# A retention-then-feed-forward kernel on one core: loads reordered between two DMA queues, weight columns interleaved, the first output block computed earlier

## The chip, the cores and the metric

The kernel runs on one core of a Trainium2 chip. The metric is the device time of one execution in microseconds (us), and the median of several runs is what counts.

## The reference

There are two parts, run one after the other. The first is a linear recurrence per batch entry and head (retention): a 64x64 state decays by a constant factor per head, takes up the outer product of k and v of each step, and is read by q. The second is a feed-forward block on all 3072 tokens.

```
q, k, v: (4, 8, 768, 64) f32;  gamma_h = 1 - 2**(-5-h)
state = gamma_h * state + k_t (outer) v_t
y_t = (1/8) * q_t @ state
x = y as (4*768, 512)
h = x @ w_in            # (512, 2048)
out = (h * cos(h)) @ w_out   # (2048, 512), f32
```

## The kernel before

The recurrence is done in chunks of 128 steps. A "pair" p (12 of them, `NP`) is one chunk of two batch entries with all 8 heads: pairs 0 to 5 are the six chunks of the first two entries, 6 to 11 those of the other two. Two pairs make a "group" g of 512 tokens (6 of them, `NG`), and a group is the unit of the feed-forward block.

Work on one pair, with the names of the code: `load` (L105) brings q, k and v for both entries from DRAM, six DMAs of 256 KB in fp32. `conv_q`, `conv_k`, `conv_v` (L150 to L165) scale them and make them bf16. `stage_t` (L167) transposes q and k on TensorE (PE) through a PSUM bank, 16 small matmuls, and copies the result to `qkt`; `stage_t_dma` (L183) does the same with two DMA transposes from the SP queue instead, and is used from pair `PT` on. `stage_a` (L196) makes the scores, 16 matmuls; `stage_m` (L211) masks them on VectorE (DVE). `stage_y` (L219) makes the outputs and the new state, and copies the outputs to `xt`, the input of the feed-forward block.

The feed-forward block has two products. F is x times `w_in`, then h*cos(h) by a Sin on ScalarE (ACT, L258) and a product on DVE (L262) into `gt`. `unit_f` (L264) does one block f of 128 of the 2048 hidden columns for the 512 tokens of a group: four matmuls of 512 columns. `pair_f` (L272) does four blocks (4r to 4r+3) for the 256 tokens of one pair: sixteen matmuls of 256 columns each; it can start when only one pair of the group is done. O is `gt` times `w_out`: `unit_o(g, j, part)` (L288) does a quarter (`part`) of the sum over f for token block j in four matmuls; after part 3 ACT copies the bank out and SP stores it.

The schedule is written out by hand: each engine runs its instructions in exactly the order in which the code issues them. There are two DMA queues for the loads: the one fed by SP ("hardware queue") and the one fed by GpSimd ("software queue", POOL). The weights come by the software queue, `w_in` in slices of 512 of its 2048 columns (L114; the first slice as two halves), `w_out` in four slices of 512 rows (L119), and are cast to bf16 on the way. Waits between engines, and for DMAs, are put in by the framework from the memory ranges that the instructions touch. It gives each queue eight DMA semaphores in rotation, so a ninth DMA of a queue is issued when the first has landed.

The order of the first third (L311 to L389): pairs 0 and 1 with idle-filling matmuls (`warm`, L313); F of both in part r=0; F of group 0 for r=1, 2, 3 as pair parts; pair 2; F of pair 2 with pair 3 between; F of pair 3. From L393 on is a loop over groups: in turn one unit of F of group g, one unit of O of group g-1, with the stages of the next pairs put between at fixed steps. The first round (g=1) has no F, only the O of group 0 with pairs 4 and 5; the second (g=2) has F of group 2 and O of group 1, and so on.

Of the kernel before, what the change touches and what calls it, by code (L numbers as in the profile page):

```python
# [30 lines left out]
def kernel(  # L31
# [9 lines left out]
    nc = tc.nc  # L41
# [8 lines left out]
    NP = B // 2 * NC  # L50
    NG = NP // 2
    PRE = 5
    PT = 5

    scale = 1.0 / math.sqrt(D)
    lg = [math.log(1.0 - 2.0 ** (-5.0 - h)) for h in range(H)]
# [48 lines left out]
    def load(eng, p, names):  # L105
        bp, c = divmod(p, NC)
        for n in names:
            t, src = SRC[n[0]]
            b = int(n[1])
            eng.dma_start(  # L110
                out=t[p % PRE][b],
                in_=src[2 * bp + b, :, ds(c * C, C)].rearrange("h t d -> t h d"))

    def load_w_in(r, n=512):  # L114
        nc.gpsimd.dma_start(
            out=w_in_sb[:, :, ts(r, n)],
            in_=moe_w_in[:, ts(r, n)].rearrange("(i p) f -> p i f", p=128))

    def load_w_out(r):  # L119
        nc.gpsimd.dma_start(  # L120
            out=w_out_sb[:, ts(r, 4), :],
            in_=moe_w_out[ts(r, 512), :].rearrange("(f p) m -> p f m", p=128))


    nc.gpsimd.iota(pos, pattern=[[C, NC]], base=1, channel_multiplier=1,
                   allow_small_or_imprecise_dtypes=True)
    load(nc.sync, 0, ("q0", "k0", "q1"))
    load(nc.sync, 1, ("q0", "q1"))
    load(nc.gpsimd, 0, ("k1", "v0", "v1"))
    make_identity(nc, ident)  # L130
    nc.vector.memset(zero, 0.0)
    nc.vector.memset(lnsc, math.log(scale))
# [17 lines left out]
    def conv_q(p, eng):  # L150
        for b in range(2):
            eng.tensor_tensor(out=qs[p % NB][:, b], in0=qf[p % PRE][b],  # L152
                              in1=bc(gq, p % NC), op=ALU.mult)

    def conv_v(p, eng):
        for b in range(2):
            eng.tensor_tensor(out=vs[p % NB][:, b], in0=vf[p % PRE][b],  # L157
                              in1=bc(gk, p % NC), op=ALU.mult)

    def conv_k(p, on_act):  # L160
        for b in range(2):
            if on_act:
                nc.scalar.copy(out=ks[p % NB][:, b], in_=kf[p % PRE][b])  # L163
            else:
                nc.vector.tensor_copy(out=ks[p % NB][:, b], in_=kf[p % PRE][b])  # L165

    def stage_t(p, split, fill=0):  # L167
        n = p % NB
        for b in range(2):
            if fill:  # L170
                warm(fill * b)
            bank = banks.take()
            tr = bank.bitcast(BF16).rearrange("p (w a t) -> p w a t", w=2, a=HP)
            for w, src in enumerate((qs[n], ks[n])):
                for a in range(HP):
                    nc.tensor.transpose(tr[:, w, a, :], src[:, b, 2 * a : 2 * a + 2, :], ident)  # L176
            if split is None or split and b == 1:
                nc.vector.tensor_copy(out=qkt[n][:, :, b], in_=tr)  # L178
            else:
                nc.scalar.copy(out=qkt[n][:, :, b], in_=tr)  # L180
            banks.give(bank)

    def stage_t_dma(p):  # L183
        n = p % NB
        for w, src in enumerate((qs[n], ks[n])):
            nc.sync.dma_start_transpose(
                out=qkt[n][:, w].rearrange("p b a t -> p (b a) t"),
                in_=src.rearrange("p b h d -> p (b h d)"))
# [75 lines left out]
    def unit_f(g, f):  # L264
        bank = banks.take()
        for i in range(KIN):
            nc.tensor.matmul(bank, lhsT=w_in_sb[:, i, ts(f, 128)], rhs=xt[g % 2][:, i, :],  # L267
                             start=(i == 0), stop=(i == KIN - 1))
        act(bank, gt[g % 2][:, f, :])
        banks.give(bank)  # L270

    def pair_f(p, r, parts=(0, 1)):  # L272

        g, hf = divmod(p, 2)
        for f in [4 * r + 2 * i for i in parts]:
            bank = banks.take()
            for e in range(2):
                for i in range(KIN):
                    nc.tensor.matmul(bank[:, ts(e, 256)], lhsT=w_in_sb[:, i, ts(f + e, 128)],  # L279
                                     rhs=xt[g % 2][:, i, ts(hf, 256)],  # L280
                                     start=(i == 0 and e == 0), stop=(i == KIN - 1),
                                     skip_group_check=True)
            act(bank, gt[g % 2][:, f : f + 2, ts(hf, 256)])
            banks.give(bank)
# [2 lines left out]

    def unit_o(g, j, part):  # L288
        if part == 0:
            o_bank[0] = banks.take()  # L290
        bank = o_bank[0]
        for f in range(4 * part, 4 * part + 4):
            nc.tensor.matmul(bank, lhsT=gt[g % 2][:, f, ts(j, 128)], rhs=w_out_sb[:, f, :],  # L293
                             start=(f == 0), stop=(f == KOUT - 1))
        if part == 3:
            o = ob[j % 4]
            bp, c = divmod(2 * g + j // 2, NC)
            dst = out[ds((2 * bp + j % 2) * S + c * C, C), :]
            if g == NG - 1 and j == 3:
                nc.vector.tensor_copy(out=o[:, ts(0, 256)], in_=bank[:, ts(0, 256)])  # L300
                nc.sync.dma_start(out=dst[:, ts(0, 256)], in_=o[:, ts(0, 256)])
                nc.scalar.copy(out=o[:, ts(1, 256)], in_=bank[:, ts(1, 256)])
                nc.scalar.dma_start(out=dst[:, ts(1, 256)], in_=o[:, ts(1, 256)])
            else:
                nc.scalar.copy(out=o, in_=bank)  # L305
                nc.sync.dma_start(out=dst, in_=o)
            banks.give(bank)
# [5 lines left out]
    def warm(n):  # L313
        for _ in range(n):
            nc.tensor.matmul(spare, lhsT=zero[:, :128], rhs=zero, start=True, stop=True,
                             skip_group_check=True)

    def masks(p, items):
        for it in items:
            stage_m(p, it)  # L320

    load(nc.gpsimd, 1, ("k0", "k1", "v0", "v1"))
    load_w_in(0, 256)
    load_w_in(1, 256)
    for r in (1, 2, 3):
        load_w_in(r)
    for p in (2, 3, 4):
        load(nc.sync, p, ("q0", "q1", "v0"))
    conv_v(1, nc.gpsimd)
    load(nc.gpsimd, 2, ("k0", "k1", "v1"))  # L330
    load(nc.gpsimd, 3, ("k0", "k1"))
    conv_q(2, nc.gpsimd)
    load(nc.gpsimd, 3, ("v1",))
    load_w_out(0)
    conv_v(2, nc.gpsimd)
    load_w_out(1)

    warm(10)
    conv_q(0, nc.vector)
# [7 lines left out]
    conv_q(1, nc.vector)  # L347
    warm(6)
    stage_y(0, nc.scalar.copy)
    conv_q(3, nc.gpsimd)  # L350
    load_w_out(2)
    load_w_out(3)
    conv_v(3, nc.gpsimd)
    load(nc.gpsimd, 4, ("k0", "k1", "v1"))
    stage_t(1, None)
    m1 = stage_a(1)
    masks(1, m1)
# [1 line left out]
    banks.give(spare)  # L359
    stage_y(1, nc.scalar.copy)  # L360
    pair_f(1, 0)
    for r in (1, 2, 3):
        pair_f(0, r)
        pair_f(1, r)
    conv_k(2, True)
    stage_t(2, None)
    m2 = stage_a(2)
    masks(2, m2)
    stage_y(2, nc.scalar.copy)
    load(nc.sync, 5, ("q0", "q1", "v0"))  # L370
    conv_q(4, nc.gpsimd)
    load(nc.gpsimd, 5, ("k0", "k1", "v1"))
    pair_f(2, 0)
    conv_k(3, True)
    pair_f(2, 1)
    stage_t(3, None)
    pair_f(2, 2, (0,))
    m3 = stage_a(3)
    masks(3, m3)
    pair_f(2, 2, (1,))  # L380
    pair_f(2, 3)
    stage_y(3, nc.scalar.copy)
    conv_v(4, nc.gpsimd)
    load(nc.sync, 6, ("q0", "q1", "v0"))
    load(nc.gpsimd, 6, ("k0", "k1", "v1"))
    for r in range(4):
        pair_f(3, r)
        if r == 2:
            conv_k(4, True)  # L389


    todo = []
    for g in range(1, NG + 1):  # L393
        for s in range(16):
            hf, r = divmod(s, 8)
            p = 2 * (g + 1) + hf
            if 1 < g < NG:
                unit_f(g, s)
            unit_o(g - 1, *divmod(s, 4))
            if p < NP:  # L400
                if r == 0 and p + 1 < NP:
                    conv_q(p + 1, nc.gpsimd)
                    conv_k(p + 1, True)
                    conv_v(p + 1, nc.gpsimd)
                elif r == 1 and p < PT:
                    stage_t(p, False)
                elif r == 2:
                    todo = stage_a(p)
                    stage_m(p, todo[0])
                    if PT <= p + 1 < NP:  # L410
                        stage_t_dma(p + 1)
                elif r == 3:
                    stage_m(p, todo[1])
                elif r == 6:
                    stage_y(p)
                    if p + 3 < NP:
                        load(nc.sync, p + 3, ("q0", "q1", "v0"))
                        load(nc.gpsimd, p + 3, ("k0", "k1", "v1"))


# [28 lines left out]
```

## Time and profile before

| what | value |
|---|---|
| median of 7 runs | 220.09 us |
| lowest and highest | 219.76 and 221.34 us |
| time of the profiled execution | 220.22 us |
| span of its trace | 218.5 us |
| mean granted TensorE clock over the span | 0.992 |
| busy PE, DVE, ACT, POOL | 92%, 52%, 53%, 38% |
| software queue (q0), hardware queue (q1) | 13.90 MB, 19.01 MB |

The span runs from the first instruction of the program to the last; 1.7 us of the execution lie around it. "Busy" of PE counts pipelined matmuls at their modelled length, so what PE loses is better seen in the distance from the start of one matmul to the start of the next. In the trace, lines such as L279 are lines of the kernel before.

### The profile page before, as it was taken

The page shows a single profiled execution, that of the slowest core. Times are in us where ns is not written, and L with a number is a line of the kernel's source. Part 1 is how long each engine was busy: PE and PEld are TensorE (multiplying, and loading weights), DVE is VectorE, ACT ScalarE, POOL GpSimd, SP SyncE. Part 2 cuts the span into 40 slices and gives each one's busy share as a digit, 9 for nine tenths or more (in the row PEclk, how much of TensorE's full clock was granted, in tenths as well). Part 3 has the DMA queues.
Part 4 walks back from the last instruction along what each step waited for, and adds up shares of the span by engine and source line. Part 5 has one row for each costly group of instructions (what it writes and reads, how often), then busy time and mean ns, then how long its engine had stood idle before and what let it go on. Part 6 is the DMA issues. An engine that isn't in the chain of part 4 may idle for free.

```text
span 218.5 us, 4249 instructions
## 1 busy us (share of the span) xinstructions
PE 201.7 (92%) x1679; PEld 112.5 (51%) x1699; DVE 113.5 (52%) x183; ACT 116.1 (53%) x185; POOL 83.9 (38%) x96
## 2 busy tenths in 40 slices
PE   7578996889999999999999999999999999999992
PEld 2246884768855454544544544544544544444440
DVE  4398588386663416557447547547546244333000
ACT  5654874748874274564474564564534644454120
POOL 7989432598799863946330520000000000000000
PEclk9799999999999999999999999999999999999999
DMA  6999999899999999998851651051011001110221
GB/s 162 330 246 196 212 314 224 172 177 282 307 207 304 293 193 314 253 231 207 206 143 52 148 144 48 3 144 50 3 48 48 20 31 48 48 49 4 96 85 59
DMA packets 62516, 33.31 MB, mean 152 GB/s; under 512 B 52320, under 2 KB 57184, under 8 KB 62496
## 3 DMA queue, kind: packets, MB, share of 16 engines
q1 hardware_dynamic: 54640, 19.01, 38.7%
q0 software_dynamic: 7712, 13.90, 25.6%
q8 instruction: 13, 0.21, 0.4%
q10 hardware_dynamic: 144, 0.13, 0.2%
q14 instruction: 7, 0.06, 0.1%
HBM read 27.26 MB, written 6.29 MB: 154 GB/s over the span
## 4 chain that ended last, share of the span: by engine, by line
PE 82%; DVE 6%; ACT 5%; DMA 3%; issue 2%; SPq 0%; DVEq 0%; ACTq 0%
PE bank L293 37%; PE bank L267 25%; PE bank L279 11%; DMA qf<-in_q_dram 3%; PE bank L205 3%; DVE am L214 2%; PE bank L228 2%; PE bank L233 2%; ACT cosb L258 1%; ACT ks L163 1%; DVE qkt L178 1%; DVE qs L152 1%; ACT xt L237 1%; PE bank L176 1%; DVE gt L262 1%
## 5 line engine op out<-in xcount | busy, mean ns | idle before, releaser
L262 DVE TENSOR_TENSOR gt<-bank,cosb 128x512 bf16<-128x512 f32 x96 | 65.9, 690 | 70.1 <-ACT cosb L258 70.0
L258 ACT ACTIVATE cosb<-bank,halfpi 128x512 bf16<-128x512 f32 x96 | 65.7, 687 | 60.1 <-PE bank L267 49.9
L293 PE MATMUL bank<-w_out_sb,gt 128*128 128x512 bf16 x377 | 93.5, 379 | 0.6 <-issue 0.3
L267 PE MATMUL bank<-xt,w_in_sb 128*128 128x512 bf16 x244 | 64.2, 379 | 1.3 <-issue 0.9
L293 PEld LDWEIGHTS <-gt 128*128 128x128 bf16 x384 | 37.2, 98 | 44.3
L267 PEld LDWEIGHTS <-w_in_sb 128*128 128x128 bf16 x256 | 24.1, 98 | 28.3
L214 DVE TENSOR_TENSOR am<-bank,mask 128x512 bf16<-128x512 f32 x48 | 30.2, 681 | 5.9 <-PE bank L205 3.3
L152 POOL TENSOR_TENSOR qs<-qf,gq 128x512 bf16<-128x512 f32 x20 | 20.6, 1051 | 31.5 <-DMA qf<-in_q_dram 29.0
L279 PE MATMUL bank<-xt,w_in_sb 128*128 128x256 bf16 x256 | 28.9, 273 | 1.4 <-ACT xt L237 1.4
L279 PEld LDWEIGHTS <-w_in_sb 128*128 128x128 bf16 x256 | 24.8, 98 | 4.4 <-issue 1.3
L157 POOL TENSOR_TENSOR vs<-vf,gk 128x512 bf16<-128x512 f32 x22 | 23.0, 1062 | 7.4 <-DMA vf<-in_v_dram 7.4
L305 ACT COPY ob<-bank 128x512 f32<-128x512 f32 x23 | 13.5, 585 | 16.3 <-PE bank L293 16.3
L110 POOL DMA_DIRECT2D kf<-in_k_dram x23 | 20.9, 912 | 0.4 <-issue 0.4
L237 ACT CAST xt<-bank 128x512 bf16<-128x512 f32 x24 | 13.1, 588 | 14.6 <-PE bank L233 14.6
L163 ACT CAST ks<-kf 128x512 bf16<-128x512 f32 x24 | 13.7, 615 | 2.6 <-DMA kf<-in_k_dram 2.6
L233 PE MATMUL bank<-am,vs 128*64 128x128 bf16 x192 | 12.2, 220 | 1.2 <-DVE am L214 1.1
L110 POOL DMA_DIRECT2D vf<-in_v_dram x14 | 12.4, 890 | 0.0
L250 DVE CAST stb<-st_ps 64x512 bf16<-64x512 f32 x12 | 8.3, 689 | 6.5 <-PE st_ps L245 6.3
L233 PEld LDWEIGHTS <-vs 128*64 128x64 bf16 x192 | 10.3, 110 | 1.8 <-issue 1.1
L228 PEld LDWEIGHTS <-stb 128*64 128x64 bf16 x160 | 8.7, 109 | 4.5 <-issue 4.2
L228 PE MATMUL bank<-qkt,stb 128*64 128x128 bf16 x160 | 10.6, 222 | 0.0
L205 PE MATMUL bank<-qkt 64*128 64x128 bf16 x192 | 8.4, 222 | 2.3 <-DVE qkt L178 1.9
(37 smaller groups left out, 68.6 us busy)
## 6 DMA issues: line engine op xcount, KB each, us to landing
qf<-in_q_dram SPq DMA_DIRECT2D x24, 256.0 KB, 6.5
kf<-in_k_dram POOLq DMA_DIRECT2D x23, 256.0 KB, 5.3
out_dram<-ob SPq DMA_DIRECT2D x23, 256.0 KB, 2.1
vf<-in_v_dram POOLq DMA_DIRECT2D x14, 256.0 KB, 6.2
vf<-in_v_dram SPq DMA_DIRECT2D x10, 256.0 KB, 7.0
w_out_sb<-in_moe_w_out_dram POOLq DMA_DIRECT2D x4, 512.0 KB, 8.9
w_in_sb<-in_moe_w_in_dram POOLq DMA_DIRECT2D x3, 512.0 KB, 14.3
w_in_sb<-in_moe_w_in_dram POOLq DMA_DIRECT2D x2, 256.0 KB, 8.0
```

Of the source, the lines that this page charges most:

```text
L110: eng.dma_start(out=t[p % PRE][b], in_=src[2 * bp + b, :, ds(c * C, C)].rearrange("h t d -> t h d"))
L152: eng.tensor_tensor(out=qs[p % NB][:, b], in0=qf[p % PRE][b], in1=bc(gq, p % NC), op=ALU.mult)
L157: eng.tensor_tensor(out=vs[p % NB][:, b], in0=vf[p % PRE][b], in1=bc(gk, p % NC), op=ALU.mult)
L163: nc.scalar.copy(out=ks[p % NB][:, b], in_=kf[p % PRE][b])
L214: nc.vector.tensor_tensor(out=am[p % 2][b][j], in0=ap[j], in1=mask.unsqueeze(1).to_broadcast([128, HP, 128]), op=ALU.mult)
L228: nc.tensor.matmul(yp[ts(j, 64), a, :], lhsT=stb[p % 2][:, b, a, ts(j, 64)], rhs=qt(n, b, a), start=True, stop=False, skip_group_check=True)
L233: nc.tensor.matmul(yp[ts(j, 64), a, :], lhsT=vs[n][:, b, 2 * a + j, :], rhs=am[p % 2][b][j][:, a, :], start=(c == 0), stop=True, skip_grou ...
L258: nc.scalar.activation(out=cb, in_=bank, func=AF.Sin, bias=halfpi)
L262: nc.vector.tensor_tensor(out=out, in0=bank, in1=cb, op=ALU.mult)
L267: nc.tensor.matmul(bank, lhsT=w_in_sb[:, i, ts(f, 128)], rhs=xt[g % 2][:, i, :], start=(i == 0), stop=(i == KIN - 1))
L279: nc.tensor.matmul(bank[:, ts(e, 256)], lhsT=w_in_sb[:, i, ts(f + e, 128)], rhs=xt[g % 2][:, i, ts(hf, 256)], start=(i == 0 and e == 0), s ...
L293: nc.tensor.matmul(bank, lhsT=gt[g % 2][:, f, ts(j, 128)], rhs=w_out_sb[:, f, :], start=(f == 0), stop=(f == KOUT - 1))
```

## The change

- **Layout of the weights.** Hidden columns are now numbered so that block f (with r = f // 4, j = f % 4) is made of the columns 512 r + 4 m + j, m = 0..127. `w_out` rows follow the same numbering, so that a partition of a `w_out` slice takes four neighbouring rows, 8 KB in one piece of DRAM, where it took four pieces of 2 KB. `w_in_sb` is filled as before, and its weight operands are read with a step of four elements through the new `w_in_t`.
- **Loads.** At the start SP issues v0 of pair 1 in place of q1 of pair 1, which goes to POOL; `iota` comes after POOL's first load. `w_in` is loaded in four slices, and all four `w_out` slices follow it on POOL, ahead of k and v of the pairs 2 to 4. For pairs 3 and 4 v0 also moves from SP to POOL.
- **Order of the work.** F of group 0 for f = 4..15 is done in `unit_f` form. O of group 0 comes right after it, ahead of and between the stages of pair 2, with two `o_bank`s at a time for j = 0, 1. The round g=1 of the loop is gone: pairs 4 and 5 with the first eight units of O of group 1 are written out ahead of the loop, and the round g=2 has the other eight at every second step. `conv_q` and `conv_v` of pair 2 and `conv_q` of pair 3 go from POOL to DVE. Two `warm` matmuls are added after pair 0. `PT` is 4, so pair 4 is transposed by DMA and no longer on PE.

```diff
-    PT = 5
+    PT = 4
...
-            in_=moe_w_out[ts(r, 512), :].rearrange("(f p) m -> p f m", p=128))
+            in_=moe_w_out[ts(r, 512), :].rearrange("(p j) m -> p j m", j=4))
+
+    w_in_f = w_in_sb.rearrange("p i (r m j) -> p i r j m", r=4, j=4)
+
+    def w_in_t(i, f):
+        return w_in_f[:, i, f // 4, f % 4, :]
...
-    load(nc.sync, 1, ("q0", "q1"))
-    load(nc.gpsimd, 0, ("k1", "v0", "v1"))
+    load(nc.sync, 1, ("q0", "v0"))
+    load(nc.sync, 2, ("q0", "q1", "v0"))
+    load(nc.gpsimd, 0, ("k1",))
...
+    load(nc.gpsimd, 0, ("v0", "v1"))
...
-            nc.tensor.matmul(bank, lhsT=w_in_sb[:, i, ts(f, 128)], rhs=xt[g % 2][:, i, :],
+            nc.tensor.matmul(bank, lhsT=w_in_t(i, f), rhs=xt[g % 2][:, i, :],
...
-                    nc.tensor.matmul(bank[:, ts(e, 256)], lhsT=w_in_sb[:, i, ts(f + e, 128)],
+                    nc.tensor.matmul(bank[:, ts(e, 256)], lhsT=w_in_t(i, f + e),
...
-    load(nc.gpsimd, 1, ("k0", "k1", "v0", "v1"))
-    load_w_in(0, 256)
-    load_w_in(1, 256)
-    for r in (1, 2, 3):
+    load(nc.gpsimd, 1, ("k0", "q1", "k1", "v1"))
+    for r in range(4):
         load_w_in(r)
-    for p in (2, 3, 4):
-        load(nc.sync, p, ("q0", "q1", "v0"))
     conv_v(1, nc.gpsimd)
+    for r in range(4):
+        load_w_out(r)
+    load(nc.sync, 3, ("q0", "q1"))
     load(nc.gpsimd, 2, ("k0", "k1", "v1"))
-    load(nc.gpsimd, 3, ("k0", "k1"))
-    conv_q(2, nc.gpsimd)
-    load(nc.gpsimd, 3, ("v1",))
-    load_w_out(0)
-    conv_v(2, nc.gpsimd)
-    load_w_out(1)
+    load(nc.gpsimd, 3, ("k0", "k1", "v0", "v1"))
+    load(nc.sync, 4, ("q0", "q1"))
+    load(nc.gpsimd, 4, ("k0", "k1", "v0", "v1"))
...
     pair_f(1, 0)
-    for r in (1, 2, 3):
-        pair_f(0, r)
-        pair_f(1, r)
+    for f in range(4, 16):
+        unit_f(0, f)
+
     conv_k(2, True)
+    conv_q(2, nc.vector)
+    conv_v(2, nc.vector)
+    for part in range(4):
+        for j in range(2):
+            unit_o(0, j, part)
+    unit_o(0, 2, 0)
+    unit_o(0, 2, 1)
     stage_t(2, None)
+    unit_o(0, 2, 2)
     m2 = stage_a(2)
     masks(2, m2)
+    conv_k(3, True)
+    unit_o(0, 2, 3)
...
+    for part in range(3):
+        unit_o(0, 3, part)
     stage_y(2, nc.scalar.copy)
+    unit_o(0, 3, 3)
+    conv_q(3, nc.vector)
...
+    attend(4)
+    o_units(1, 0, 4)
+    later(4)
+    attend(5)
+    ahead(6)
+    stage_t_dma(6)
+    o_units(1, 4, 8)
+    later(5)
```

More of the change, by code (lines that the diff above doesn't have):

```diff
@@ L121, in load_w_out @@
             out=w_out_sb[:, ts(r, 4), :],
-            in_=moe_w_out[ts(r, 512), :].rearrange("(f p) m -> p f m", p=128))
+            in_=moe_w_out[ts(r, 512), :].rearrange("(p j) m -> p j m", j=4))
+    w_in_f = w_in_sb.rearrange("p i (r m j) -> p i r j m", r=4, j=4)
+    def w_in_t(i, f):
+        return w_in_f[:, i, f // 4, f % 4, :]
+    load(nc.sync, 0, ("q0", "k0", "q1"))
+    load(nc.sync, 1, ("q0", "v0"))
+    load(nc.sync, 2, ("q0", "q1", "v0"))
+    load(nc.gpsimd, 0, ("k1",))
     nc.gpsimd.iota(pos, pattern=[[C, NC]], base=1, channel_multiplier=1,
                    allow_small_or_imprecise_dtypes=True)
-    load(nc.sync, 0, ("q0", "k0", "q1"))
-    load(nc.sync, 1, ("q0", "q1"))
-    load(nc.gpsimd, 0, ("k1", "v0", "v1"))
+    load(nc.gpsimd, 0, ("v0", "v1"))
     make_identity(nc, ident)
@@ L289, in unit_o @@
         if part == 0:
-            o_bank[0] = banks.take()
-        bank = o_bank[0]
+            o_bank[j] = banks.take()
+        bank = o_bank[j]
         for f in range(4 * part, 4 * part + 4):
@@ L349 @@
     stage_y(0, nc.scalar.copy)
[L350 to L354, printed above, removed]
+    warm(2)
     stage_t(1, None)
@@ L361, with attend, ahead, later @@
     pair_f(1, 0)
-    for r in (1, 2, 3):
-        pair_f(0, r)
-        pair_f(1, r)
+    for f in range(4, 16):
+        unit_f(0, f)
     conv_k(2, True)
+    conv_q(2, nc.vector)
[5 more added lines that the diff above has]
+    unit_o(0, 2, 1)
     stage_t(2, None)
+    unit_o(0, 2, 2)
     m2 = stage_a(2)
     masks(2, m2)
+    conv_k(3, True)
+    unit_o(0, 2, 3)
+    load(nc.sync, 5, ("q0", "q1", "v0"))
+    load(nc.gpsimd, 5, ("k0", "k1", "v1"))
+    for part in range(3):
+        unit_o(0, 3, part)
     stage_y(2, nc.scalar.copy)
-    load(nc.sync, 5, ("q0", "q1", "v0"))
+    unit_o(0, 3, 3)
+    conv_q(3, nc.vector)
+    conv_v(3, nc.gpsimd)
     conv_q(4, nc.gpsimd)
-    load(nc.gpsimd, 5, ("k0", "k1", "v1"))
+    conv_v(4, nc.gpsimd)
     pair_f(2, 0)
-    conv_k(3, True)
+    stage_t(3, None)
     pair_f(2, 1)
-    stage_t(3, None)
-    pair_f(2, 2, (0,))
     m3 = stage_a(3)
     masks(3, m3)
-    pair_f(2, 2, (1,))
+    conv_k(4, True)
+    stage_t_dma(4)
+    load(nc.sync, 6, ("q0", "q1", "v0"))
+    load(nc.gpsimd, 6, ("k0", "k1", "v1"))
+    pair_f(2, 2)
     pair_f(2, 3)
     stage_y(3, nc.scalar.copy)
[L383 to L386, printed above, removed]
-        pair_f(3, r)
[L388 to L393, printed above, removed]
+    conv_q(5, nc.gpsimd)
+    conv_v(5, nc.gpsimd)
+    pair_f(3, 0)
+    conv_k(5, True)
+    stage_t_dma(5)
+    for r in range(1, 4):
+        pair_f(3, r)
+    def attend(p):
+        todo = stage_a(p)
+        masks(p, todo)
+    def ahead(p):
+        if p < NP:
+            conv_q(p, nc.gpsimd)
+            conv_k(p, True)
+            conv_v(p, nc.gpsimd)
+    def later(p):
+        stage_y(p)
+        if p + 3 < NP:
+            load(nc.sync, p + 3, ("q0", "q1", "v0"))
+            load(nc.gpsimd, p + 3, ("k0", "k1", "v1"))
+    def o_units(g, a, b):
+        for u in range(a, b):
+            unit_o(g, *divmod(u, 4))
+    attend(4)
[6 more added lines that the diff above has]
+    later(5)
+    for g in range(2, NG + 1):
         for s in range(16):
@@ L396 @@
             p = 2 * (g + 1) + hf
-            if 1 < g < NG:
+            if g < NG:
                 unit_f(g, s)
-            unit_o(g - 1, *divmod(s, 4))
+            if g > 2:
+                unit_o(g - 1, *divmod(s, 4))
+            elif s % 2:
+                unit_o(1, *divmod(8 + s // 2, 4))
             if p < NP:
[L401 to L406, printed above, removed]
+                if r == 0:
+                    ahead(p + 1)
                 elif r == 2:
@@ L409 @@
                     stage_m(p, todo[0])
-                    if PT <= p + 1 < NP:
+                    if p + 1 < NP:
                         stage_t_dma(p + 1)
@@ L414 @@
                 elif r == 6:
[L415 to L418, printed above, removed]
+                    later(p)
 _INS = ['q', 'k', 'v', 'moe_w_in', 'moe_w_out']
```

## Prediction

> **What bounds the kernel now.** I first read the page's engine rows and its slices. PE is busy nearly throughout, so the time is PE's work plus the places where PE waits; these lie in the first third, where the DMA engines are full.
>
> ```profile
> span 218.5 us, 4249 instructions
> PE 201.7 (92%) x1679; PEld 112.5 (51%) x1699; DVE 113.5 (52%) x183; ACT 116.1 (53%) x185; POOL 83.9 (38%) x96
> ...
> PE   7578996889999999999999999999999999999992
> ...
> DMA  6999999899999999998851651051011001110221
> ```
>
> Then PE's matmul rows in order of time, from the trace's timeline (start, length, operation, count, wait before). They give the prices: 112 pair-part matmuls start at 21.69 and the next operation starts at 33.92, so 12.23/112 = 109 ns each and 1.75 us for a part of 16. The transposes of pair 2 start at 33.92 and its scores, outputs and state end only at 40.75.
>
> ```profile
> 21.69 12.39 PE L279 MATMUL bank<-xt,w_in_sb 128*128 128x256 bf16 x112 [0.47 <-ACT xt L237]
> 33.92 0.39 PE L176 MATMUL bank<-ident,qs 128*128 128x128 bf16 x4
> ...
> 35.37 0.40 PE L176 MATMUL bank<-ident,ks 128*128 128x128 bf16 x4 [1.06 <-ACT ks L163]
> ...
> 40.75 0.49 PE L279 MATMUL bank<-xt,w_in_sb 128*128 128x256 bf16 x3 [0.42 <-ACT xt L237]
> ```
>
> Third, the view of the tile `w_in_sb`. The last of its five DMAs is issued at 11.6 and lands 16.9 later, at 28.5. PE uses the first columns at 18.0, so each slice is used as it lands. A load of these weights takes 98 ns.
>
> ```profile
> L279 PEld LDWEIGHTS <-w_in_sb x128: 95/98/99, 18.0 to 33.7; 128*128 128x128 bf16 x128
> L279 PE MATMUL bank<-xt,w_in_sb x128: 269/273/283, 18.0 to 33.8; 128*128 128x256 bf16 x128
> L115 POOL DMA_DIRECT2D w_in_sb<-in_moe_w_in_dram x5: 777/784/795, 8.7 to 11.6; - x5
> ...
> DMA to landing us min/median/max: 7.3/11.6/16.9
> ```
>
> The same rows give the other prices: a unit of F or O (four matmuls of 512 columns, 216 ns apart) 0.86 us; transposes T of a pair 0.89; scores A 0.55; outputs and state Y 1.13 (0.88 without state).
>
> [...]
> - [...] after the gaps from 5.2 to 8.5, three warm matmuls take 1.28 us (427 ns apart, against 216 later), and the rate is full by 12.9, 4.4 us after work resumed.
> - [...] No row of the trace shows a strided weight load.
> - [...] the q load issued at 14.6 landed 25.9 us later.
>
> **The change, part by part.**
>
> *A wait for all of w_in (decides the sign).* In the built program of the kernel before, the weight loads of `w_in_sb` wait for one DMA at a time, the next slice's only when its blocks come up. In the changed program the first weight load of `pair_f(0, 0)` (i=0) waits for the first slice, and the second (i=1) waits for the software queue's semaphores 0, 1 and 2. Counting POOL's loads in order, these are the slices 2, 3 and 4; PE reads nothing else that they carry, and no later weight load waits for a slice. The interleaved view is tracked as a range that touches every slice's rectangle. So PE stops one matmul into F until all of `w_in` is in. Behind that instruction stands all of PE's program, and with it ACT's and DVE's.
> When is that? Before: 28.5. The software queue has seven loads ahead of it as before, but the first slice now comes in 1024 B packets (96 ns each in the trace's packet records) rather than 512 B (59 ns): per DMA engine 32 x 96 = 3.07 against 64 x 59 = 3.78, 0.7 less[...]. I take 27.6, bounds 26.9 and 28.6. The second load came at 18.15 before, so the delay is +9.45. (The opening is otherwise alike: 12 loads ahead on both queues, `iota` later by one load issue of 1.05 but hidden behind k0, which lands at 6.0; the two `warm` lie in the wait for `conv_q(1)`.)
>
> *Cold clock.* [...] By the 4.4 us above, of which about 4 at half rate, it loses about half of that: +1.8, bounds 1.2 and 2.5.
>
> *PE's content.* From 21.69 to 78.54, where the second round begins, before does 15 pair parts (26.2), 16 O units (13.8), 3 T, 4 A, 3 Y with state and one without (9.2): 49.2 of 56.85, so 7.65 were waits. After does from the same point to its round g=2: 9 pair parts (15.75), 12 F units (10.35), 24 O units (20.7), 2 T, 4 A, the Ys (8.3): 55.1. Eight of the O units (6.9) are then missing in the round, so 48.2: -1.0.
>
> *Waits that go.* Of the 7.65, the order removes those around pair 2 (6.83 for 2.57 of work: 4.3), pair 3 and pairs 4, 5. O units stand between T, A and Y. What is late next: A(2) behind its `qkt` copies, 0.25; `xt` after Y(3), 0.67 as now; `xt` after Y(5), which no O covers any more, 0.6; A(3) 0.1; small gaps in O (16 units at 222 instead of 216 ns) 0.6. Together 2.2, so -5.45; it could be -6.2, or -3 if a load is late.
>
> *Moved loads and queues.* w_out follows w_in: 4 x 3.1 us [...], so all in at about 40. It is first used after F: 27.6 + 3.65 (the stretch 18.04 to 21.69) + 1.8 - 0.1 + 1.75 + 10.35 = 45: five us of cover. With F not delayed it would have cost about 1.8. Then k, v of pair 2 at 0.82 us per load (the spacing of such landings now) are in by 43, pair 4's by 50. On POOL the compute behind these issues starts late, conv_v(3), but PE needs it after 66. On SP the hardware queue starves: [...] q1 of pair 3 lands at about 53; DVE's `conv_q(3)` comes at 59 and hides it. Six conversions on DVE (0.69 each) lie beside O. Pair 4's DMA transposes (landing in 3 to 8 us) come some 10 us early; pair 6's only about 2 us, behind load 7 on SP: 0, bounds 0 and +2.
>
> *Sum.* 9.45 + 1.8 - 1.0 - 5.45 = +4.8. Against the profiled execution: span 218.5 to 223.3, time 220.22 to 225.0; the median is 0.13 lower, so 224.9. From the bounds: 222.6 to 228.2.
>
> **The rivals.**
> - *It goes faster (the wait doesn't bind).* If PE could take each slice as it lands, there is neither the 9.45 nor the 1.8, but the w_out wait of 1.8 comes: 220.1 - 1.0 - 5.45 + 1.8 + 0.3 = 215.8. It decides if PE resumes before 27.6 - 4.8 = 22.8. The 4.2 MB would have to come in about 9 us after 14, 470 GB/s, where the page's slices show at most 330. For it speaks only that the list of waits could name an earlier use of those semaphores. 4%.
> - *Strided weight loads are slow.* In F units 216 ns cover a load of twice 98; in pair parts 109 ns do not. 10 parts x 16 x (196 - 109) = +13.9: 238.8. [...] no row excludes it. Cost taken 0, bounds 0 and 13.9. 12%.
> - *A late transfer takes the place of the waits* (pair 6's transposes, q of pair 3): +2 to 3, 227.5. 14%.
> - *Everything cancels:* resume at 26.9, little cold time, no new wait and a quicker O: 220 to 221. 3%.
>
> **How the numbers follow.** The forecast has 67% (222.6 to 226.5), the late transfer is inside the range, the strided loads are outside. Differences under 0.3% (0.66 us) can't be told from none here. Faster 4%, within 3%, slower 93%.
>
> **What would show it.** Right: one gap on PE from about 18.1 to 27.6 at the first F matmuls, ended by a `w_in` DMA; half-rate matmuls for some 4 us; then no wait on `w_out`, and few gaps to 88. Weight loads of `w_in_sb` at 98 ns, pair parts at 109. Wrong: PE running through F at 18 to 34, weight loads near 200, or gaps later than 54 that end with a q DMA or a DMA transpose.

## The result, and the profile after

The changed kernel takes 226.81 us (median of 12 runs, 226.1 to 227.25), beside 220.26 us for the kernel before (median of 31 runs in the same session, 219.31 to 222.94). The ratio is 1.0283, 95% interval 1.0261 to 1.0305: slower. Ratios here and below use only the executions within 1.5% of the fastest of their kernel, medians and ranges use all of them. The profiled execution of the changed kernel took 227.12 us with a span of 225.4, 6.9 us more than the span before. Numbers of lines such as L286 are from here on those of the kernel that is spoken of; in the changed kernel L286 is the matmul of `pair_f` (L279 before), L274 that of `unit_f`, L300 that of `unit_o`.

The page first: head, engines, and three of the slice rows.

```profile
span 225.4 us, 4119 instructions
PE 201.7 (90%) x1615; PEld 114.2 (51%) x1637; DVE 115.9 (51%) x189; ACT 113.6 (50%) x183; POOL 77.5 (34%) x91
...
PE   7760099999999999899999999999999999999992
...
PEclk9997559999999999999999999999999999999998
DMA  6999999993795958999999623132011011110212
```

PE is busy for the same 201.7 us as before; the 6.9 us more are time in which it is not busy. A slice is 5.6 us, and the fourth and fifth digits of the PE row, 0 and 0, are a hole at about 17 to 28 us that the row of before did not have. The granted clock falls in the same place (7, 5, 5). To the right of the hole the row is fuller: it has a single 8, in slice 17, where the row of before had a 6 and two 8s in slices 7 to 9.

PE's rows in order of time show the edges of the hole (start, length, operation, count, and in brackets the wait ahead of it).

```profile
17.23 0.30 PE L286 MATMUL bank<-xt,w_in_sb 128*128 128x256 bf16 x1 [1.31 <-DMA w_in_sb<-in_moe_w_in_dram]
28.42 3.36 PE L286 MATMUL bank<-xt,w_in_sb 128*128 128x256 bf16 x15 [10.88 <-DMA w_in_sb<-in_moe_w_in_dram]
...
34.13 1.91 PE L286 MATMUL bank<-xt,w_in_sb 128*128 128x256 bf16 x16 [0.43 <-ACT xt L244]
35.87 0.81 PE L274 MATMUL bank<-xt,w_in_sb 128*128 128x512 bf16 x2
```

One matmul of F runs as soon as the first slice is in. The second, which reads columns of the same first slice, waits 10.88 us for a `w_in` DMA. The 15 that then follow start over 3.29 us, 219 ns apart; the next part (34.13 to 35.87) has its 16 at 109 ns.

The view of the tile `w_in_sb` says what was awaited. The four loads are issued from 8.8 to 11.0 and the last is in 17.2 us later, at 28.28: that is the end of the hole. It also gives the duration of the weight loads, whose step is now four elements.

```profile
L274 PEld LDWEIGHTS <-w_in_sb x48: 112/113/117, 35.8 to 45.8; 128*128 128x128 bf16 x48
...
L286 PEld LDWEIGHTS <-w_in_sb x32: 112/114/152, 17.2 to 35.7; 128*128 128x128 bf16 x32
...
L115 POOL DMA_DIRECT2D w_in_sb<-in_moe_w_in_dram x4: 775/780/790, 8.8 to 11.0; - x4
...
DMA to landing us min/median/max: 8.4/13.3/17.2
```

Last the list of PE's waits (total, times, longest), and the busy times by stretch (PE, PEld, DVE, ACT, POOL, then granted clock, DMA share and GB/s). The waits for `qs`, `ks` and `qkt` that headed the list before (2.5, 2.4 and 1.9 us) are down to 1.2 and less; one entry has taken their place.

```profile
PE bank L286 <- DMA w_in_sb<-in_moe_w_in_dram: 12.2, 2, 10.9
PE bank L322 <- DVE gt L138: 1.3, 1, 1.3
PE bank L183 <- DVE qs L159: 1.2, 1, 1.2
PE bank L286 <- ACT xt L244: 1.2, 2, 0.8
```

```profile
17.20:28.40 11.20, 0.30 (x1) 0.13 (x2) 0.65 (x2) 0.00 (x0) 2.69 (x3) 0.60 1.21 201
28.40:34.13 5.73, 5.29 (x64) 4.10 (x65) 1.38 (x2) 2.60 (x5) 2.00 (x3) 0.59 1.06 209
34.13:92.12 57.99, 56.06 (x555) 38.33 (x560) 37.32 (x58) 36.02 (x60) 32.32 (x35) 1.00 0.85 220
```

In the first stretch PE is busy for 0.30 of the 11.20 us, DVE for 0.65 and ACT not at all: they stand behind PE. POOL only issues three loads (2.69), and the DMA share stays high. In the second the granted clock is 0.59. The third, which holds everything that the change rearranged, is at full clock and PE is busy in 97% of it.

### The profile page after: what moved, and what is told of

The parts are those of the page before. It is cut to its first block, busy times and chain, and to the rows that moved or that the text cites. A ratio compares the mean times of both kernels' runs of the same rounds, so it can differ in the third digit from the quotient of the medians.

```text
span 225.4 us, 4119 instructions
## 1 busy us (share of the span) xinstructions
PE 201.7 (90%) x1615; PEld 114.2 (51%) x1637; DVE 115.9 (51%) x189; ACT 113.6 (50%) x183; POOL 77.5 (34%) x91
## 4 chain that ended last, share of the span: by engine, by line
PE 81%; DMA 8%; POOL 4%; ACT 2%; issue 2%; DVE 2%; another core or an unknown queue 0%; DVEq 0%; POOLq 0%; ACTq 0%
PE bank L300 37%; PE bank L274 29%; DMA w_in_sb<-in_moe_w_in_dram 8%; PE bank L286 7%; PE bank L212 2%; PE bank L235 2%; PE bank L240 2%; POOL kf L110 1%; POOL vf L110 1%; DVE am L221 1%; ACT xt L244 1%; POOL w_in_sb L115 1%; PE bank L183 1%; PE st_ps L252 1%; ACT cosb L265 1%
## 5 line engine op out<-in xcount | busy, mean ns | idle before, releaser
L300 PE MATMUL bank<-w_out_sb,gt 128*128 128x512 bf16 x377 | 92.2, 379 | 0.5 <-issue 0.2
L274 PE MATMUL bank<-xt,w_in_sb 128*128 128x512 bf16 x290 | 74.0, 379 | 2.0 <-issue 0.9
L300 PEld LDWEIGHTS <-gt 128*128 128x128 bf16 x384 | 37.2, 98 | 43.6
L274 PEld LDWEIGHTS <-w_in_sb 128*128 128x128 bf16 x304 | 33.6, 114 | 30.7 <-issue 0.7
L286 PE MATMUL bank<-xt,w_in_sb 128*128 128x256 bf16 x160 | 20.2, 287 | 13.4 <-DMA w_in_sb<-in_moe_w_in_dram 12.2
L159 POOL TENSOR_TENSOR qs<-qf,gq 128x512 bf16<-128x512 f32 x16 | 16.4, 1041 | 35.9 <-DMA qf<-in_q_dram 35.9
L286 PEld LDWEIGHTS <-w_in_sb 128*128 128x128 bf16 x160 | 17.8, 116 | 14.9 <-issue 12.2
L110 POOL DMA_DIRECT2D kf<-in_k_dram x23 | 20.7, 903 | 10.3 <-DMA w_in_sb<-in_moe_w_in_dram 6.2
L164 POOL TENSOR_TENSOR vs<-vf,gk 128x512 bf16<-128x512 f32 x20 | 20.6, 1046 | 2.3 <-DMA vf<-in_v_dram 2.1
L110 POOL DMA_DIRECT2D vf<-in_v_dram x15 | 13.3, 887 | 6.5 <-DMA w_out_sb<-in_moe_w_out_dram 4.0
L235 PE MATMUL bank<-qkt,stb 128*64 128x128 bf16 x160 | 10.9, 230 | 0.0
L322 PE MATMUL bank<-gt 128*128 128x512 bf16 x20 | 7.3, 506 | 1.3 <-DVE gt L138 1.3
```

Source lines behind the costliest of these rows:

```text
L110: eng.dma_start(out=t[p % PRE][b], in_=src[2 * bp + b, :, ds(c * C, C)].rearrange("h t d -> t h d"))
L235: nc.tensor.matmul(yp[ts(j, 64), a, :], lhsT=stb[p % 2][:, b, a, ts(j, 64)], rhs=qt(n, b, a), start=True, stop=False, skip_group_check=True)
L274: nc.tensor.matmul(bank, lhsT=w_in_t(i, f), rhs=xt[g % 2][:, i, :], start=(i == 0), stop=(i == KIN - 1))
L286: nc.tensor.matmul(bank[:, ts(e, 256)], lhsT=w_in_t(i, f + e), rhs=xt[g % 2][:, i, ts(hf, 256)], start=(i == 0 and e == 0), stop=(i == KIN ...
```

## The experiments

The theory: the single interleaved tile makes a weight load wait for every slice of `w_in`, and that wait, with the cold clock after it, costs more than the reordering gains. The rivals: the order of the loads delays `w_in` itself; the reordering gains less than was reckoned; the strided weight loads cost.

**Plain columns in the changed kernel.** Everything stays, except that block f is again made of neighbouring columns and `w_out` is read as before.

```diff
     def w_in_t(i, f):
-        return w_in_f[:, i, f // 4, f % 4, :]
+        return w_in_sb[:, i, ts(f, 128)]
...
-            in_=moe_w_out[ts(r, 512), :].rearrange("(p j) m -> p j m", j=4))
+            in_=moe_w_out[ts(r, 512), :].rearrange("(f p) m -> p f m", p=128))
```

> The changed kernel with the hidden columns numbered as before (w_in_t gives w_in_sb[:, i, ts(f, 128)], w_out again four 2 KB rows a partition); loads and order stay changed. Theory (the interleaved view makes PE wait for all of w_in): the gap of 11.0 us at the first F matmuls goes, and with it the half-rate stretch, 2.3; first slice used at about 17.3. w_out then becomes the wait, with slices 3.4 us apart from 28.3, in by 41.8, against a need at 38.0: +2 to 3.5. Together 215.5 to 217.5, clearly under the kernel before. Rival (the reordered loads or the late pair 2 cost the time, the gap only hides it): 222 or more, with new DMA waits between 33 and 60. Rival (strided weight loads, 113 ns against 98, cost): about 2 us less than the changed kernel only, and the gap stays.

Measured: 217.36 us (216.97 to 217.8), ratio to before 0.9851 (0.9782 to 0.992), span 215.5. The slices land as in the changed kernel (17.05 to 28.20), yet no wait for `w_in` is left: the first sixteen matmuls of F run through. PE waits for `w_out` instead, whose last slice now lands at 41.64.

```profile
17.70 1.92 PE L284 MATMUL bank<-xt,w_in_sb 128*128 128x256 bf16 x16
```

```profile
PE bank L298 <- DMA w_out_sb<-in_moe_w_out_dram: 2.7, 2, 1.4
```

So the order of the loads is not the cause, and the reordering without the interleaved layout is a gain, though of less than 2%.

**The kernel before with the interleaved layout alone.** The converse: only the view of one tile and the 8 KB rows of `w_out`, put into the kernel before, with its own order.

```diff
-            in_=moe_w_out[ts(r, 512), :].rearrange("(f p) m -> p f m", p=128))
+            in_=moe_w_out[ts(r, 512), :].rearrange("(p j) m -> p j m", j=4))
...
+    w_in_f = w_in_sb.rearrange("p i (r m j) -> p i r j m", r=4, j=4)
...
-            nc.tensor.matmul(bank, lhsT=w_in_sb[:, i, ts(f, 128)], rhs=xt[g % 2][:, i, :],
+            nc.tensor.matmul(bank, lhsT=w_in_t(i, f), rhs=xt[g % 2][:, i, :],
```

> The kernel before with only the interleaved columns (the view w_in_t on one tile, w_out rows 8 KB a partition). Theory: PE waits at 18.1 until 28.5 for all of w_in, +10.4, and +2.3 of half rate; the waits around pairs 2 and 3 are waits between engines and stay: 220.3 + 12.7 = 233, down to 230 if some of them were waits for DMAs. That the order of the changed kernel gives back about 6 us shows by the distance to it. Rival (the order and loads of the changed kernel are what is slow): about 220, no gap.

Measured: 234.09 us (232.3 to 235.17), ratio 1.0601 (1.0509 to 1.0694), span 231.5: 13.0 more than before. The hole is the same, 10.3 us and then a part at half rate, and the waits for the conversions stay.

```profile
PE bank L284 <- DMA w_in_sb<-in_moe_w_in_dram: 10.3, 1, 10.3
PE bank L181 <- ACT ks L168: 2.4, 2, 1.4
```

The layout in one tile by itself costs some 13 us. With the plain one, the rest of the change gains about 3 us. The two halves of the change are thus shown apart.

**The interleaved layout in four tiles.** If it is the tracking of one tile, and not the layout, then a tile for each slice should end the wait without giving up the 8 KB rows.

```diff
-    w_in_sb = sb([128, KIN, DF], BF16, "w_in_sb")
+    w_in_r = [sb([128, KIN, 512], BF16, f"w_in{r}_sb") for r in range(4)]
...
+    w_in_f = [t.rearrange("p i (m j) -> p i j m", j=4) for t in w_in_r]
...
-        return w_in_f[:, i, f // 4, f % 4, :]
+        return w_in_f[f // 4][:, i, f % 4, :]
```

> The changed kernel with w_in_sb made of four tiles, one for each slice, the columns interleaved inside each; same memory, same loads, same matmuls and order. Theory (only the tracking of the view makes PE wait): each weight load waits for its own slice, no gap at 17.3 to 28.3, no half rate; w_out in at 38.9 against a need at 38.0, and q of pair 3, which landed at 50.8 and 51.6, about 1 us late: about 215.0, 214 to 217. Rival (the stride itself or the DMA order is at fault): 222 or more. Weight loads of w_in_sb stay at 113 ns, pair parts at 109 ns a matmul; if a pair part grows to 114 ns or more, the stride costs time too.

Measured in the changed kernel: the profiled execution took 215.51 us, span 213.8, without a wait for `w_in` and without one for `w_out` (slices in at 30.99 to 39.00, O from 33.77).

```profile
17.99 1.94 PE L286 MATMUL bank<-xt,w_in_sb 128*128 128x256 bf16 x16
```

But three further executions took 220.01, 220.05 and 220.85. The hole was settled. The spread of 5 us was new, and with it four executions give no time for this kernel.

The same in the kernel before, to see what the strided weight loads cost where they are the only difference:

> The kernel before with the interleaved columns and four w_in tiles, so the stride and the 8 KB rows of w_out without the wait for all of w_in. Theory (the stride is hidden, only the wait costs): weight loads of w_in_sb 114 ns in place of 98, pair parts still 109 ns a matmul, no gap at 18: 220.3, within 0.5%, against 234 for the same layout on one tile. Rival (the stride costs where 256-column matmuls follow each other): 256 pair-part matmuls at 114 ns, +1.3, up to 222.

Measured: 221.28 us (220.2 to 225.28, 12 runs), beside 220.15; ratio 1.0027 (0.9994 to 1.006). No cost can be told from none. The rows of PE's weight loads (count, busy us and mean ns) and of the 112 pair-part matmuls show why:

```profile
L298 PEld LDWEIGHTS <-gt 128*128 128x128 bf16 x384 | 37.2, 98 | 43.3
L272 PEld LDWEIGHTS <-w_in_sb 128*128 128x128 bf16 x256 | 28.0, 114 | 25.5
L284 PEld LDWEIGHTS <-w_in_sb 128*128 128x128 bf16 x256 | 27.8, 113 | 1.6 <-issue 1.3
```

A strided load takes 113 to 114 ns where the plain one of the same size (`gt`) takes 98, but the 112 matmuls from 21.46 on took 12.22 us, 109 ns each, as with plain columns.

**The hole filled with idle matmuls.** To separate the cold clock from the wait, `warm(44)` in the changed kernel keeps PE at work while it waits.

```diff
     masks(1, m1)
+    warm(44)
     pair_f(0, 0)
```

> The changed kernel with 44 idle-filling matmuls ahead of pair_f(0, 0), 44 x 216 ns = 9.5 us in the gap; nothing else. Theory (clock): PE stays at full rate, the first pair part takes 1.75 and not 3.4 us after the gap, the end of w_in stays at 28.3: 2.0 to 2.3 less than the changed kernel, 224.6. Rival (the slow start after the gap has another cause, such as DMA traffic into the same memory): no change, 226.8.

Measured: 225.25 us (224.67 to 226.5), ratio 1.0227 (1.0135 to 1.0319). The span of the profiled execution is 223.0, 2.4 less than that of the changed kernel. The medians lie only 1.6 apart and the intervals of the two ratios overlap, so the size of the gain rests on the two traces.

```profile
16.19 9.44 PE L322 MATMUL bank<-gt 128*128 128x512 bf16 x43 [0.16 <-issue]
25.47 0.27 PE L286 MATMUL bank<-xt,w_in_sb 128*128 128x256 bf16 x1
28.13 1.80 PE L286 MATMUL bank<-xt,w_in_sb 128*128 128x256 bf16 x15 [2.39 <-DMA w_in_sb<-in_moe_w_in_dram]
```

The 15 matmuls now take 1.80 us instead of 3.36. The next part starts at 31.67 instead of 34.13: 2.46 earlier, of which 0.29 is the resume (28.13 against 28.42) and 2.17 the clock. The wait itself, which stays, is the larger part.

**Where the spread comes from.** This goes beyond the change itself: it asks what limits the kernel once the hole is gone. Three readings were tried. First, that loads left on the hardware queue come too late now and then: v0 of pair 2 and q of pair 3 were moved to the software queue, in four tiles.

```diff
-    load(nc.sync, 2, ("q0", "q1", "v0"))
+    load(nc.sync, 2, ("q0", "q1"))
...
-    load(nc.sync, 3, ("q0", "q1"))
-    load(nc.gpsimd, 2, ("k0", "k1", "v1"))
-    load(nc.gpsimd, 3, ("k0", "k1", "v0", "v1"))
+    load(nc.gpsimd, 2, ("k0", "k1", "v0", "v1"))
+    load(nc.gpsimd, 3, ("q0", "k0", "q1", "k1", "v0", "v1"))
```

> The kernel of four tiles with v0 of pair 2 and q0, q1 of pair 3 moved from the hardware to the software queue, among the loads of their pairs. In the four-tile kernel's trace these landed at 41.4, 48.9 and 51.3 on the starved hardware queue, with v0 of pair 2 needed at about 41 and q of pair 3 at about 48. Theory (its executions at 220 rather than 215.5 are those in which these come later still): here they land in order at about 41 to 46, and all executions come near 215, spread under 1%. Rival (the spread comes from elsewhere, or three more loads ahead make k of pair 3 late): some executions stay at 220.

Measured: 217.95 us (215.45 to 220.55, 6 runs), ratio 0.9822 (0.9759 to 0.9886). The spread is as wide as it was, so this reading fell. Second, the unaltered four tiles again, to catch a long execution in a profile:

> The kernel of four tiles once more, for its spread (215.5 in one execution, 220.0 to 220.9 in three). Theory (late loads of the hardware queue): values between 215 and 221, and if the profiled one is high, its trace has a PE gap of 4 to 5 us between 40 and 60 that goes back to v0 of pair 2 or q of pair 3. Rival (the chip was disturbed then): all near 215.5. Second rival: all near 220, and no such gap.

Measured: 217.96 us (216.12 to 221.8, 7 runs), ratio 0.9868 (0.9815 to 0.9921). The profiled execution took 221.01, and PE's waits in it, and the two places, are these:

```profile
PE bank L212 <- DMA qkt<-ks: 4.4, 2, 2.2
```

```profile
76.20 0.62 PE L212 MATMUL bank<-qkt 64*128 64x128 bf16 x16 [2.18 <-DMA qkt<-ks]
...
87.91 0.62 PE L212 MATMUL bank<-qkt 64*128 64x128 bf16 x16 [2.18 <-DMA qkt<-ks]
...
90.12 1.92 PE L300 MATMUL bank<-w_out_sb,gt 128*128 128x512 bf16 x4
```

The scores of pairs 5 and 6 wait for their DMA transposes, and the eight matmuls after the second wait run at half rate (88.46 to 91.83, 3.37 us in place of 1.73). SP's queue shows how the transposes become late: two loads of q ahead of pair 5's transposes occupied SP for 6.93 us, and the transpose of q behind them was issued at 68.33 and landed 7.00 later. In the execution of 215.51 the same two loads occupied SP for 2.41 us.

```profile
59.07 6.93 SPq L110 DMA_DIRECT2D qf<-in_q_dram  x2
66.05 2.11 SPq L110 DMA_DIRECT2D vf<-in_v_dram  x1
68.33 3.77 SPq L193 DMA_TRANSPOSE qkt<-qs  x1
```

Third, then, two kernels that take these transposes from behind the loads. Both start from the kernel with the moved loads of the first reading. In one, pairs 5 and 6 are transposed on PE:

```diff
     conv_k(5, True)
-    stage_t_dma(5)
...
     attend(4)
+    stage_t(5, None)
     o_units(1, 0, 4)
...
-    stage_t_dma(6)
...
+                elif r == 1 and p == 6:
+                    stage_t(p, None)
```

> The kernel with the loads in order, and pairs 5 and 6 transposed on PE instead of by DMA (32 matmuls more, 2 x 0.89 us). Theory (late DMA transposes make the spread): no PE wait on a transfer between 60 and 95, every execution 216 to 218, spread under 1%. Rival: spread 215 to 221 as before with PE gaps elsewhere.

In the other, their conversions and DMA transposes are put ahead of the loads of pairs 6 and 7 in SP's and POOL's order:

```diff
+    conv_q(5, nc.gpsimd)
+    conv_v(5, nc.gpsimd)
+    conv_k(5, True)
+    stage_t_dma(5)
     load(nc.sync, 6, ("q0", "q1", "v0"))
     load(nc.gpsimd, 6, ("k0", "k1", "v1"))
...
     attend(4)
+    ahead(6)
+    stage_t_dma(6)
     o_units(1, 0, 4)
     later(4)
     attend(5)
-    ahead(6)
-    stage_t_dma(6)
```

> The kernel with the loads in order, and pair 5's conversions and DMA transposes put ahead of load 6, pair 6's ahead of load 7, on POOL, ACT and SP. The four-tile kernel's slow execution (221.0) had PE waiting 4.4 us for DMA transposes of pairs 5 and 6, then 8 matmuls at half rate (427 ns, +1.7); its fast one (215.5) waited 0.7. Theory (late transposes behind loads make the spread): these waits fall under 0.5 us in all executions, 214.5 to 216, spread under 1%. Rival (the transposes are slow whatever stands ahead, because any DMA traffic slows them): spread up to 220 stays.

Measured: on PE 217.28 us (217.16 to 217.98, 6 runs), ratio 0.9855 (0.982 to 0.989); the spread is gone, at the price of PE's own transposes (two times 0.89 us). Ahead of the loads 214.36 us (214.27 to 216.6, 6 runs), ratio 0.9737 (0.9689 to 0.9785): four executions at 214.27 to 214.41, two at 216.5. So late DMA transposes made most of the spread. The two profiled executions of the four tiles agree: between 215.51 and 221.01 us the waits for transposes grew from 0.7 to 4.4 us, and the half rate added 1.6. The kernel with the transposes ahead is faster than both kernels of this document.

Of the two at 216.5 one was profiled. PE waits 1.9 us there at pair 3's transposes, for DVE's conversion of q; the two operations of that conversion took 7.65 us together, the second of them alone 7.05, where others of the same kind take 0.68. During the second of them POOL ran six conversions back to back.

```profile
46.98 7.65 DVE L159 TENSOR_TENSOR qs<-qf,gq 128x512 bf16<-128x512 f32 x2
```

```profile
48.02 2.05 POOL L164 TENSOR_TENSOR vs<-vf,gk 128x512 bf16<-128x512 f32 x2
50.03 2.04 POOL L159 TENSOR_TENSOR qs<-qf,gq 128x512 bf16<-128x512 f32 x2
52.04 2.03 POOL L164 TENSOR_TENSOR vs<-vf,gk 128x512 bf16<-128x512 f32 x2
```

That the one held up the other is a guess from this coincidence. The last run gives this conversion to POOL, so that the two do not meet:

```diff
-    conv_q(3, nc.vector)
+    conv_q(3, nc.gpsimd)
     conv_v(3, nc.gpsimd)
```

> The kernel of the run with the earlier transposes, with one edit: the conversion of q of pair 3 goes to GpSimd, ahead of conv_v(3) there, and no longer to VectorE. In the two longer executions of that run (216.5 against 214.3) PE waited 1.9 us for this one VectorE operation, which took 7.05 us instead of 0.68 beside six GpSimd conversions in a row. If the two engines hold each other up there, all executions should now be at 214.3 within 0.4, with no wait of PE above 1 us at the transposes of pair 3. Rival: the 216.5 come from something else (the loads), and still appear in about a third of the executions; or GpSimd's conversion comes too late by itself (about 1 us more than on VectorE), and every execution is at 215 to 216.

Measured: 214.72 us (214.2 to 217.79, 8 runs), ratio 0.9702 (0.9648 to 0.9756). Half right: no wait at pair 3's transposes is left and no DVE conversion is stretched, but longer executions are still there (215.86, 216.97, 217.79). The profiled one, 216.97, shows two other losses:

```profile
17.69 3.45 PE L286 MATMUL bank<-xt,w_in_sb 128*128 128x256 bf16 x16 [1.38 <-DMA w_in_sb<-in_moe_w_in_dram]
21.07 0.25 PE L235 MATMUL bank<-qkt,stb 128*64 128x128 bf16 x2
```

```profile
PE bank L212 <- DMA qkt<-ks: 1.1, 1, 1.1
```

The wait of 1.38 us is for the first slice of `w_in`. It is not what sets this execution apart, for the run with transposes on PE has it too (1.30 us). But here the sixteen matmuls after it run at half rate: they take 3.38 us (17.69 to 21.07), and 1.86 there. That is 1.5 us, and the late transposes at 111.86 are 1.1; together they are the 2.6 us between this execution and the shortest ones. The two kernels can't be told apart by their times.

## Why the prediction was right, and which of its terms were off

The mechanism and the sign were right, and the time lies in the range, 1.9 us above the number given. It lies above 226.5, though, in the part of the range that the prediction kept for a late transfer, and no such transfer came: three terms inside their bounds erred in the same direction. (The range is also not what the bounds add up to, which would be 222.8 to 231.0.) Term by term as the prediction divides the time, from the two traces:

| term | predicted us | measured us | from |
|---|---|---|---|
| second F matmul | +9.45 | +10.27 | 28.42 against 18.15 |
| cold clock | +1.8 | +2.17 | from there to the next part: 5.71 against 3.54 |
| content of PE and waits that go | -6.45 | -5.77 | 57.99 (34.13 to 92.12) less 8 x 0.864 for eight O units, against 56.85 |
| the rest | 0 | +0.23 | 133.28 and the eight O units, against 139.96 |
| sum | +4.8 | +6.9 | spans 225.4 and 218.5 |

- *The wait for all of w_in.* Right, and shown from three sides: it goes with plain columns or with four tiles, and comes to the kernel before with one interleaved tile. The size was short by 0.8. The step that was off is "I take 27.6": the first slice did come sooner (17.18, against 18.16 for its second half before), but the last one landed at 28.28 against 28.54, only 0.26 sooner instead of the 0.9 reckoned with (0.7 of it from packet times, the rest the author's estimate). The gap from the first to the second slice grew from 3.65 to 4.37 us; what took the time back was not tried apart. In the eight experiments with the changed loads of `w_in` the last slice landed between 27.28 and 28.46, in the two with the loads of before at 28.63 and 28.69: sooner, but mostly by less than was reckoned.
- *Cold clock.* Right in kind, 0.37 short. The run with the filled hole confirms it: with PE kept busy, this stretch is 2.17 us shorter. That the hole would bring half rate was the author's estimate; the trace shows it, for after 10.9 us without work 15 matmuls came at 219 ns instead of 109, and the full rate was back only by 33.2, 4.8 us after the resume. The 4.4 us that the prediction started from was read too late: in the kernel before, matmuls of 512 columns are 216 ns apart from 11.75 on, so half rate ended within 3.3 us of 8.48. After the hole in the kernel before with the interleaved layout it lasted 3.9 us (28.76 to 32.7). The length thus differs from case to case, and that 1.8 came so near to 2.17 is in part luck.
- *PE's content and the waits.* With the content at -1.0 as worked out, the waits fell by 4.77 instead of 5.45: 2.9 us of them are left and not 2.2. They are where they were named (0.99 from the last state matmul to F after Y(3), 0.94 after Y(5)); the rest is small losses of about 0.1 us each in parts and units.
- *Moved loads.* Better than predicted: a `w_out` slice takes 2.65 us and not 3.1 (3.1 was an estimate by bytes, from the 96 ns of a 1024 B packet), all are in at 38.94, and O starts at 46.23. The cover was 7 us. Without the hole there is nearly none, yet the wait of 1.8 that was stated for that case is small with the 8 KB rows (four tiles: none in one profiled execution, 0.4 in the other), while it does come with 2 KB rows (plain columns: 2.7). The late q1 of pair 3 (issued at 16.5, in at 50.76, 34.3 later; 53 was the author's estimate) was hidden as said.
- *Weight loads.* "Weight loads of `w_in_sb` at 98 ns" was wrong: 113 to 114. That a step of four would leave them at 98 was the author's estimate, for the trace before has no strided load. No cost in time could be told: the 256-column matmuls still came 109 ns apart. How loads of 113 ns fit between these was not tried. The rival of 13.9 us did not occur.
- *Pair 6's transposes.* "0, bounds 0 and +2": 0 in the profiled execution of the changed kernel, where they landed at 94.59 and the scores of pair 6 started at 95.67; and its 12 executions lie within 1.2 us. The risk was real all the same. Where the hole is gone the same transposes, and pair 5's, cost 4.4 us of waiting in the profiled long execution. That the hole gives the loads 12 us to get ahead of PE, and so covers them, is argued from this, and not shown.
- *The faster rival* was put at 215.8 with 1.8 us for `w_out`. The version without the wait took 215.51 at its best and 217.96 in the median of seven, so as a price of the other side it was near; its condition was false, since PE did wait. One argument against it was wrong: the 4.2 MB are `w_in` in fp32, but the trace counts the weights as they arrive, in bf16 (37 loads of 0.262 MB and twice 2.1 MB make the 13.90 MB of the software queue). In that measure 2.1 MB in 9 us are 233 GB/s, which the 330 of the page do not exclude.

## What to carry to other kernels

Before a weight tile that is filled in slices is read through a rearranged view, look in the built program for what the first reader waits: here a view that is tracked as a range over all slices made it wait for the last DMA (10.88 us), and with one tile per slice the sixteen matmuls ran through from 17.99 on. While that reader was held at the front of PE, the engines behind it stood too (of 11.20 us DVE was busy for 0.65 and ACT for 0.00), so the wait of 10 us was paid in full, and the cold clock came on top with 2.2. When a hole is closed, look again at the transfers that it may have covered: here DMA transposes behind bulk loads on the same queue were next, and their place ahead of the loads was worth 3.6 us in the median (217.95 to 214.36), where the four tiles had brought 8.85 (226.81 to 217.96).

## What was not expected of the hardware

- Weight loads with a step of four bf16 take 113 to 114 ns instead of 98.
- One DVE conversion of 128x512 from fp32 took 7.05 us instead of 0.68 beside six POOL conversions in a row. No conversion was stretched so when it ran on POOL; whether the one held up the other was not measured.
- In the profiled long execution of the four tiles the DMA transposes that were issued between 55 and 81 us, beside bulk loads, landed after 4.0 to 11.6 us, and those from 111 us on after 2.7 to 4.3. Two q loads of 256 KB occupied SP for 6.93 us at issue.
- PE ran at half rate for 3.4 us after a wait of 1.38 us (the last run) and after one of 2.18 (pair 6, four tiles), and kept its rate after waits of 1.30 (transposes on PE), 2.18 (pair 5, four tiles) and 2.39 (filled hole). The length of the last wait alone does not decide it.
